# Attention and a routed FFN on one core: rests of the task list after the token choice set to 13 slots and 3 slots

## The chip, the core and the metric

One NeuronCore of a Trainium2 chip runs the whole program in one launch. The metric is the device time of one execution in microseconds (us).

## The reference

Eight batches of 3136 tokens, model width 256. The output of the attention goes through a routed FFN that touches the 128 best tokens of each batch:

```
scores = (z @ z.T) / S                     # z: [8, 3136, 64]
x = u * (max(scores, 0)**2 @ v)            # u, v: [8, 3136, 256]
s = x @ w_gate                             # one score for each token
top = the 128 tokens of a batch with the highest s
h = max(x[top] @ w1, 0)                    # w1: [256, 1024]
x[top] = x[top] + sigmoid(s[top]) * (h @ w2)   # w2: [1024, 256]
```

All products are in float32 accuracy: each operand is split into a high and a low part (names that end in `hi`, `h`, `H` and in `lo`, `l`, `L`), and three products of the parts are summed.

## The kernel before

**Slots.** The work of a batch is cut into 7 chunks of query columns: chunks 0 to 4 have 512 columns, chunk 5 has 256, chunk 6 has 320. Each chunk is worked through in 13 slots, 91 slots for a batch and 728 in all. A slot takes two blocks of 128 keys (the last one of a chunk half a block) and sums their share of the chunk's output on TensorE: the function `mix` issues 12 matmuls (4 in the last slot) at line 521, `acc<-hi,V`, `acc<-lo,V` and `acc<-hi,Vr` by the profile's names. The last slot of a chunk is the one with `Vr`. A slot of 512 columns is long, a slot of chunk 5 is half as long.

**Old and new squares.** The matrix of scores is symmetric. A new pair of key blocks is scored on TensorE (line 415, `sc<-Z,ZH` and `sc<-Z,ZL`), squared on ScalarE and VectorE, and its transposed copy is stored to DRAM (`squares`, `squares_narrow`, `squares_own`). A later chunk fetches that copy instead of computing it (`qk<-squares`, lines 364, 369 and 372), three buffers deep. Chunk 5 and chunk 6 are mostly old squares: they need few scores and many fetches. Scores and squares of a slot are issued three slots ahead of its `mix`.

**Queues.** All plain DMAs of the loop stand in one queue, SyncE's (SP), in program order. SP issues a DMA when what it needs is free or there, and everything behind it waits as well. GpSimd (POOL) issues the two indirect DMAs of the FFN, the gather of the chosen tokens (`xe<-out,ids`) and the scatter of their new values (`out<-y,ids`, line 1158).

**The task list.** Work beside the attention is a list of tasks, `far`. A task has some TensorE operations, which `mix` spreads among the 12 matmuls of a slot, some operations for after that slot, and, as a third member, its rest: the number of slots until the next task of the list may be taken (2 where none is named; 1 in the last batch). At the end of a batch, `route` puts 30 to 40 slots of choosing tokens into the list (counting, then `ahead` at line 795 with `quotas` and `spans`, then `take` at line 836, which needs the spans' result `of` from line 832), and behind that the FFN. So the choice and the FFN of one batch run inside the chunks of the next.

**The FFN.** Its tasks, in order: `number` (the tokens' row numbers; with it SP gets the load of the two halves of w1, 1 MB each, `wh<-w1h_there` and `wl<-w1l_there`, line 185), `gather`, an empty task, `weigh`, the transposition of the tokens (`xeT`, line 1078), six matmuls `h` of 512 columns (line 1104), their transposition `hT` (four matmuls, line 1120), the second six of `h`, then a task that only queues the load of the two halves of w2 into the same two buffers (`wh<-w2h_there`, `wl<-w2l_there`, 1 MB each), the second `hT`, and last 24 matmuls `y` of 256 columns (line 1148) with the scatter. The first four `y` read `wh`, the next four `wl`, and so on.

**Which batches.** The FFNs of batches 0 to 4 run in the next batch in this way. Batches 5 and 6 (`put_off`) only choose, gather and transpose there; their FFNs run at the very end beside that of batch 7, whose routing has rules of its own. So batch 6 runs its seven chunks with no `h`, `hT` and `y` in them.

In batches 1 to 5 the FFN before stands in chunks 3 to 5: `number` at slot 0 of chunk 3, `gather` at slot 3, `weigh` at slot 8, `xeT` at slot 10; the first `h` at slot 0 of chunk 4, `hT` at slot 3, the second `h` at slot 6, the load of w2 behind slot 8, the second `hT` at slot 10; `y` at slot 0 of chunk 5.

Of the kernel before, what the change touches and what calls it, by code (L numbers as in the profile page):

```python
# [85 lines left out]
def attention_then_routed_ffn(ctx: ExitStack, tc: tile.TileContext, zt, ut, v, wg, w1, w2, cst, cst16, keys, outs, at, cap):  # L86
# [260 lines left out]
    def spend(act=0.0, dve=0.0, pool=0.0):  # L347
        busy["act"] += act
        busy["dve"] += dve
        busy["pool"] += pool  # L350
# [187 lines left out]
    def put_off(b):  # L538
        return B - 1 - HELD <= b < B - 1 and merged(B - 1) > 0

    def merged(b):
        return LATE if b == B - 1 and 0 < cap <= P else 0
# [121 lines left out]
    def route(b):  # L664
# [59 lines left out]
        def settle(rd):  # L724
            junk = moe.tile([TP, NS], F32, name="enough", tag="enough")[:R]
            m = moe.tile([TP, 1], F32, name="m", tag="m")[:R]
            nc.vector.tensor_scalar(
                junk, st["ps"][:R, :NS], float(cap), None, op0=ALU.is_ge, op1=ALU.add, accum_out=m
            )
            mi = moe.tile([TP, 1], I32, name="mi", tag="mi")[:R]  # L730
            nc.vector.tensor_copy(mi, m)
            base = moe.tile([TP, 1], I32, name="base", tag="base", bufs=2)[:R]
            if rd == last:
                base = st["ps"][:R, 64:65].bitcast(I32)
            if rd == 0:
                k = moe.tile([TP, 1], I32, name="place", tag="place")[:R]
                nc.vector.tensor_scalar(
                    k, mi, 32 - BITS, INT_MIN, op0=ALU.logical_shift_left, op1=ALU.bitwise_xor
                )
                flip = moe.tile([TP, 1], I32, name="flip", tag="flip")[:R]  # L740
                nc.vector.tensor_scalar(
                    flip, k, 31, 0x7FFFFFFF, op0=ALU.arith_shift_right, op1=ALU.bitwise_and
                )
                nc.vector.tensor_tensor(base, k, flip, op=ALU.bitwise_xor)
            else:
                nc.vector.tensor_scalar(
                    base, mi, 32 - BITS * (rd + 1), st["base"], op0=ALU.logical_shift_left, op1=ALU.bitwise_xor
                )
            st["base"] = base
            spend(dve=0.6)  # L750
# [69 lines left out]
        def spans(r0):  # L820

            rank = consts["rank"][:R, r0 : r0 + P]
            taken, begin, end = st["taken"], st["begin"], st["end"]
            if r0:
                nc.vector.tensor_scalar(taken[:, NT : NT + 1], begin, -float(r0), -2.0 * NT, op0=ALU.add, op1=ALU.max)
                nc.vector.tensor_scalar_min(taken[:, NT : NT + 1], taken[:, NT : NT + 1], 2.0 * P)
            else:
                nc.vector.tensor_scalar_min(taken[:, NT : NT + 1], begin, 2.0 * P)
            upper = moe.tile([TP, P], F32, name="upper", tag="upper")[:R]
            nc.vector.tensor_scalar(upper, rank, end, None, op0=ALU.is_le)  # L830
            of = moe.tile([TP, P], BF16, name="of", tag="big", bufs=2)[:R]
            nc.vector.scalar_tensor_tensor(of, rank, begin, upper, op0=ALU.is_gt, op1=ALU.mult)
            st["of"] = of
            spend(dve=0.6)
# [6 lines left out]
        tasks = [([fold], [start, count], 3)]  # L841
# [4 lines left out]
        if late:  # L846
            tasks.append(([total], [lambda: settle(last), masks]))
            tasks += [([columns], keep_columns), ([places], ranks)]
            tasks += choose(st, 0, cap)
            choice[b] = st  # L850
        else:
            tasks.append(([total], [lambda: settle(last), masks, run_up]))
            tasks.append(([ahead], [quotas, lambda: spans(0)]))
            for r0 in range(0, cap, P):
                n = min(P, cap - r0)
                first, *ffn = expert(b, st, n, r0)
                if put_off(b) and b == B - 2:
                    tasks = [(*t[:2], 2) for t in tasks]
                if r0:
                    tasks.append(([], lambda r0=r0: spans(r0)))  # L860
                tasks.append(([take], None))
                tasks += first
                if put_off(b):
                    held.append(ffn)
                else:
                    tasks += ffn[0] + ffn[1]
# [13 lines left out]
    def choose(st, r0, n):  # L880

        R, NT = st["G"].shape
        QT = Q // 4
        NP = NT // QT

        def pick(q):
            oh = moe.tile([TP, QT, P], BF16, name="oh", tag="big", bufs=2)[:R]
            t = slice(q * QT, (q + 1) * QT)
            nc.vector.tensor_tensor(
                oh,  # L890
                consts["rank"][:R, r0 : r0 + P].rearrange("p (o r) -> p o r", o=1).broadcast_to([R, QT, P]),
                st["rk"][:, t].rearrange("p (t o) -> p t o", o=1).broadcast_to([R, QT, P]),
                op=ALU.is_equal,
            )
            st["oh", q] = oh
            spend(dve=1.1)

        def find(q):
            if q == 0:
                st["ps"] = misc_bank("ids")  # L900
            what = st["what"]
            for i in range(QT):
                t = q * QT + i
                nc.tensor.matmul(
                    st["ps"][:, : what.shape[2]], st["oh", q][:, i, :], what[:, t, :],
                    start=(t == 0), stop=(t == NT - 1),
                )

        def begin():
            tok = consts["tok_half16"][:R].rearrange("p (t w) -> p t w", w=2)  # L910
            what = moe.tile([TP, NT, 5], BF16, name="what", tag="what")[:R]
            nc.vector.tensor_copy(what[:, :, :2], tok)
            cut(st["G"], what[:, :, 2:])
            st["what"] = what
            pick(0)

        tasks = [([], begin), ([], lambda: pick(1))]
        for q in range(NP):
            then = (lambda q=q: pick(q + 2)) if q + 2 < NP else None
            tasks.append(([lambda q=q: find(q)], then))  # L920
        tasks[-1] = (tasks[-1][0], lambda: keep_choice(st))
        return tasks
# [408 lines left out]
    for k, (b, c, js, is_old) in enumerate(slots):  # L1331
# [5 lines left out]
        tasks = []  # L1337
# [58 lines left out]
        if len(js) == 1 and cap > 0:  # L1396
            if c == NCH - 1 - late:
                far.extend([None, *route(b)])
            elif c >= NCH - late:
                last_merge = merge(b, c)  # L1400
                far.extend([None, *last_merge])
                if c == NCH - 1:
                    first, ffn, more = expert(b, choice[b], cap)
# [60 lines left out]
```

## Time and profile before

| | |
|---|---|
| time, median of 3 runs | 2114.52 us (2112.32 to 2115.31) |
| time of the profiled execution | 2112.72 us |
| its span, first to last instruction | 2110.9 us |
| TensorE busy with matmuls | 2081.4 us, 99% of the span |
| VectorE, ScalarE, GpSimd busy | 1559.2, 1263.3, 1313.5 us |
| DMA | 412.01 MB, mean 195 GB/s |
| granted TensorE clock | 1.000 |

A page of the profile names each group of instructions by line, engine, operation and tiles; an arrow `<-` behind a number names what ended a wait. Times in a timeline are us from the start of the span; `x4` behind a row merges four like instructions that follow each other, and the duration is then that of all four. Matmuls overlap each other, so one row's duration is not the distance between two starts.

### The profile page before, as it was taken

How to read it: one execution, taken by the hardware profiler on the slowest of the kernel's cores; microseconds unless marked ns; L12 is line 12 of the kernel's file. 1: busy time of each engine (PE TensorE's matmuls, PEld its weight loads, DVE VectorE, ACT ScalarE, POOL GpSimd, SP SyncE). 2: the span in 40 equal slices, each digit the busy share in tenths (PEclk: the TensorE clock that was granted, in tenths of full speed). 3: DMA queues.
4: the chain of work that ended last, by engine and by line, in shares of the span. 5: the costliest groups of instructions: out<-in, count | busy, mean ns of one | idle time of the engine just before them, and what ended most of it. 6: DMA issues, size and time to landing. Idle time of an engine off the chain costs nothing.

```text
span 2110.9 us, 31339 instructions
## 1 busy us (share of the span) xinstructions
PE 2081.4 (99%) x10359; PEld 1750.4 (83%) x10359; DVE 1559.2 (74%) x2361; ACT 1263.3 (60%) x1570; POOL 1313.5 (62%) x703
## 2 busy tenths in 40 slices
PE   8999999999999999999999999999999999999999
PEld 6788978889888898888888888888888888887788
DVE  8766678775877668776678767787577876788776
ACT  7665576554766457654576546765467654775543
POOL 6676577645766458664587646766467655666643
PEclk9999999999999999999999999999999999999999
DMA  6698766787668766688666876678766776666862
GB/s 189 202 261 222 198 184 173 217 199 213 181 186 218 202 195 190 188 220 220 177 190 187 229 211 173 190 195 217 210 182 185 196 193 171 203 188 162 220 173 96
DMA packets 425730, 412.01 MB, mean 195 GB/s; under 512 B 147616, under 2 KB 338912, under 8 KB 421984
## 3 DMA queue, kind: packets, MB, share of 16 engines
q1 hardware_dynamic: 424512, 407.66, 69.8%
q0 software_dynamic: 768, 2.10, 0.3%
q8 instruction: 81, 1.33, 0.3%
q14 instruction: 81, 0.66, 0.1%
q10 hardware_dynamic: 288, 0.26, 0.0%
HBM read 235.31 MB, written 172.23 MB: 193 GB/s over the span
## 4 chain that ended last, share of the span: by engine, by line
PE 74%; DVE 6%; DMA 6%; ACT 5%; POOL 3%; issue 3%; SPq 2%; POOLq 0%; ACTq 0%; DVEq 0%
PE acc L521 60%; PE sc L415 12%; DVE a L436 2%; POOL lo L485 2%; ACT a L425 2%; ACT hi L426 2%; DMA vst<-in_v 2%; DMA qk<-squares_narrow 1%; DVE aT L454 1%; DMA wl<-w2l_there 1%; DVE lo L485 1%; DMA squares_narrow<-aT 1%; PE h L1104 1%; PE y L1148 1%; SPq L265 0%
## 5 line engine op out<-in xcount | busy, mean ns | idle before, releaser
L521 PE MATMUL acc<-hi,V 128*128 128x512 f32 (+2 forms) x5376 | 1226.0, 366 | 9.0 <-ACT hi L393 4.7
L485 POOL TENSOR_TENSOR lo<-a,hi 128x1024 fp32r<-128x1024 f32 (+2 forms) x327 | 740.8, 2268 | 609.3 <-DVE a L436 438.9
L521 PEld LDWEIGHTS acc<-hi,V 128*128 128x128 f32 x5376 | 930.3, 188 | 175.9 <-DVE ut L566 9.1
L521 PE MATMUL acc<-lo,V 128*128 128x512 f32 (+2 forms) x2688 | 664.2, 364 | 7.2 <-POOL lo L485 3.5
L425 ACT ACTIVATE a<-sc 128x1024 f32<-128x1024 f32 (+4 forms) x408 | 363.2, 890 | 493.2 <-PE sc L415 374.9
L521 PEld LDWEIGHTS acc<-lo,V 128*128 128x128 f32 x2688 | 471.4, 188 | 89.0 <-DVE lo L485 6.4
L436 DVE TENSOR_TENSOR a<-sc,a 128x1024 f32<-128x1024 f32 (+3 forms) x335 | 339.9, 1015 | 258.1 <-ACT hi L426 227.9
L393 ACT CAST hi<-qk 128x1024 fp32r<-128x1024 f32 (+2 forms) x320 | 274.4, 862 | 254.5 <-PE acc L521 204.5
L485 DVE TENSOR_TENSOR lo<-qk,hi 128x1024 fp32r<-128x1024 f32 (+2 forms) x230 | 348.2, 1523 | 84.4 <-ACT hi L393 83.2
L454 DVE STREAM_TRANSPOSE aT<-a 128x512 f32<-128x512 f32 (+1 forms) x520 | 341.0, 691 | 89.5 <-ACT a L431 62.7
L426 ACT ACTIVATE hi<-a 128x1024 fp32r<-128x1024 f32 (+4 forms) x408 | 377.4, 925 | 21.4 <-PE acc L521 5.0
L415 PE MATMUL sc<-Z,ZH 128*128 128x512 f32 (+2 forms) x760 | 280.8, 373 | 3.7 <-DVE a L436 2.1
L415 PE MATMUL sc<-Z,ZL 128*128 128x512 f32 (+2 forms) x760 | 278.2, 370 | 0.7 <-DVE ZL L121 0.7
L485 POOL TENSOR_TENSOR lo<-qk,hi 128x512 fp32r<-128x512 f32 (+2 forms) x90 | 172.9, 1924 | 61.1 <-issue 45.5
L415 PEld LDWEIGHTS sc<-Z,ZH 128*128 128x128 f32 x760 | 142.6, 188 | 35.0 <-DVE a L436 7.7
L415 PEld LDWEIGHTS sc<-Z,ZL 128*128 128x128 f32 x760 | 142.6, 188 | 25.3 <-DVE ZL L121 1.1
L121 POOL TENSOR_TENSOR V<-vst,V 128x512 fp32r<-128x512 f32 x89 | 128.2, 1445 | 28.5 <-ACT V L120 22.4
L587 POOL TENSOR_TENSOR ut<-x,w_run 128x1024 f32<-128x1024 f32 (+2 forms) x52 | 124.3, 2390 | 26.5 <-DVE x L578 25.7
L121 POOL TENSOR_TENSOR ZL<-zst,ZH 128x512 fp32r<-128x512 f32 (+2 forms) x56 | 69.4, 1244 | 17.1 <-ACT ZH L120 17.1
L431 ACT ACTIVATE a<-a 128x1024 f32<-128x1024 f32 x73 | 77.5, 1062 | 2.3
L120 ACT CAST V<-vst 128x512 fp32r<-128x512 f32 x95 | 57.7, 608 | 30.0 <-DMA vst<-in_v 30.0
L566 DVE SCALAR_TENSOR_TENSOR ut<-acc,ut 128x512 f32<-128x512 f32 (+2 forms) x112 | 64.1, 613 | 12.6 <-PE acc L521 12.4
(173 smaller groups left out, 1054.6 us busy)
## 6 DMA issues: line engine op xcount, KB each, us to landing
squares<-aT SPq DMA_DIRECT2D x160, 512.0 KB
qk<-squares SPq DMA_DIRECT2D x320, 256.0 KB
squares_narrow<-aT SPq DMA_DIRECT2D x320, 128.0 KB
qk<-squares_narrow SPq DMA_DIRECT2D x80, 512.0 KB
vst<-in_v SPq DMA_DIRECT2D x190, 128.0 KB
out<-x SPq DMA_DIRECT2D x162, 128.0 KB
ut<-in_ut SPq DMA_DIRECT2D x40, 512.0 KB
squares_own<-aT SPq DMA_DIRECT2D x39, 256.0 KB
```

What stands on the lines that cost most here:

```text
L121: (lo_on or nc.vector.tensor_tensor)(lo, src, hi.bitcast(F32), op=ALU.subtract)
L393: nc.scalar.copy(by(hi), src)
L415: nc.tensor.matmul(ps[:, q], z[:, j * P : (j + 1) * P], mov, start=z is ZH, stop=z is ZL)
L425: nc.scalar.activation(a, ps[:, :n], AF.Relu)
L426: nc.scalar.activation(pieces[0][0](hi), pieces[0][1], AF.Square)
L431: nc.scalar.activation(a, a, AF.Square)
L436: square = lambda: nc.vector.tensor_tensor(a[rows], ps[rows, :n], a[rows], op=ALU.mult)
L454: nc.vector.transpose(to, a[rows, q].rearrange("p (m t a) -> p m t a", t=GT, a=Q))
L485: on.tensor_tensor(view(lo), src, view(hi).bitcast(F32), op=ALU.subtract)
L521: nc.tensor.matmul(ac[h], w, mov, start=first and h not in started, stop=stop)
L566: nc.vector.scalar_tensor_tensor(xT[:, h, :w], acc[b, c][h], SCALE * SCALE, xT[:, h, :w], op0=ALU.mult, op1=ALU.mult)
L587: nc.gpsimd.tensor_tensor(wx, runs, consts["wg_run"].rearrange("p (o r) -> p o r", o=1).broadcast_to([P, NB, RUN]), op=ALU.mult,)
```

## The change

Two rests in the function `route` are set, for all batches but the last. The task `ahead` gets 3 slots of rest in place of 2, and the task `take` gets 13 in place of 2, but stays at 2 where the FFN is put off (batches 5 and 6). For batch 6 the rests of the earlier tasks were set to 2 already, which stays so; its `take`, which runs in the last batch, had the 1 slot of that batch and now has 2.

```
-            tasks.append(([ahead], [quotas, lambda: spans(0)]))
+            tasks.append(([ahead], [quotas, lambda: spans(0)], 3))
...
-                tasks.append(([take], None))
+                tasks.append(([take], None, 2 if put_off(b) else 13))
```

In batches 1 to 5 `take` moves from slot 10 of chunk 2 to slot 11, `number` from slot 0 of chunk 3 to slot 11 of chunk 3, `gather` to slot 0 of chunk 4, `weigh` to slot 6, `xeT` to slot 8, the first `h` to slot 10 of chunk 4; the first `hT` to slot 0 of chunk 5, the second `h` to slot 3, the load of w2 to behind slot 6, the second `hT` to slot 8, and `y` to slot 10 of chunk 5. In batch 6 only `take` moves. The slots of the attention themselves stay as they are.

The end of the FFN on TensorE, before. The rows with 128x512 end chunk 4 (`Vr` is its last slot), those with 128x256 begin chunk 5:

```order
L521 MATMUL acc<-lo,V 128x512 x4
L1120 MATMUL hT<-c_sb,hr 128x128 x4
L521 MATMUL acc<-hi,V 128x512 x8
L521 MATMUL acc<-lo,V 128x512 x4
L521 MATMUL acc<-hi,Vr 128x512 x4
L521 MATMUL acc<-hi,V 128x256 x3
L1148 MATMUL y<-wh,hh 128x256 x2
L521 MATMUL acc<-hi,V 128x256
L1148 MATMUL y<-wh,hh 128x256 x2
L521 MATMUL acc<-lo,V 128x256
L1148 MATMUL y<-wl,hh 128x256 x3
```

The same place of the FFN now, three slots before the end of chunk 5:

```order
L521 MATMUL acc<-lo,V 128x256 x4
L1120 MATMUL hT<-c_sb,hr 128x128 x4
L521 MATMUL acc<-hi,V 128x256 x8
L415 MATMUL sc<-Z,ZH 128x256
L415 MATMUL sc<-Z,ZL 128x256
L521 MATMUL acc<-lo,V 128x256 x4
L521 MATMUL acc<-hi,V 128x256 x3
L1148 MATMUL y<-wh,hh 128x256 x2
L521 MATMUL acc<-hi,V 128x256
L1148 MATMUL y<-wh,hh 128x256 x2
L521 MATMUL acc<-hi,V 128x256
L1148 MATMUL y<-wl,hh 128x256 x3
```

The matmuls `y` moved from the first slot of chunk 5 to its eleventh, and all slots between the load of w2 and `y` are now slots of 256 columns.

On SP, the queue of plain DMAs, before, from the end of chunk 4 on. `squares_narrow_4` are stores of chunk 4, `qk<-squares_narrow_2`, `_3` and `_4` fetches for chunk 5, `out<-x` the output of chunk 4, `Z<-ZH` and `Z<-ZL` the columns of chunk 6, the later `qk` rows fetches for chunk 6, `ut` the input u for chunk 5:

```order
L468 DMA squares_narrow_4_111<-aT 32x4x256 x4
L185 DMA wh<-w2h_there 128x2048
L185 DMA wl<-w2l_there 128x2048
L468 DMA squares_narrow_4_111<-aT 32x4x128 x2
L369 DMA qk<-squares_narrow_2_107 128x2x512
L369 DMA qk<-squares_narrow_3_109 128x2x512
L223 DMA zst<-in_zt 64x512 x2
L369 DMA qk<-squares_narrow_4_111 128x2x512
L585 DMA out<-x 32x16x64 x4
```

The same queue now, from that `out<-x` on:

```order
L585 DMA out<-x 32x16x64 x4
L265 DMA Z<-ZH 64x4x32 x2
L267 DMA Z<-ZH 64x64
L265 DMA Z<-ZL 64x4x32 x2
L267 DMA Z<-ZL 64x64
L369 DMA qk<-squares_narrow_0_103 128x2x512
L372 DMA qk<-squares_narrow_0_103 128x256
L185 DMA wh<-w2h_there 128x2048
L185 DMA wl<-w2l_there 128x2048
L556 DMA ut<-in_ut 128x2x256
L369 DMA qk<-squares_narrow_1_105 128x2x512
L372 DMA qk<-squares_narrow_1_105 128x256
```

The load of w2 moved back past the fetches and stores of chunk 5 and past the first fetch for chunk 6; before, the `ut` row followed that fetch directly.

The load of w1 on the same queue, as a difference, in chunk 3 and at the start of chunk 4:

```order
-L185 DMA wh<-w1h_there 128x2048
-L185 DMA wl<-w1l_there 128x2048
 L364 DMA qk<-squares_2_106 32x4x512 x4
 L460 DMA squares_3_108<-aT 512x1x256
@@ -172,4 +170,6 @@
 L468 DMA squares_narrow_3_109<-aT 32x4x128 x2
 L364 DMA qk<-squares_2_106 32x4x512 x4
+L185 DMA wh<-w1h_there 128x2048
+L185 DMA wl<-w1l_there 128x2048
 L475 DMA squares_own_4_121<-aT 128x512
 L383 DMA vst<-squares_own_4_121 32x4x128 x4
```

It moved from before the third fetch of chunk 3 to before the store and the fetch back of `squares_own` of chunk 4.

## The prediction

> **What bounds the kernel now.** I read the page first, then TensorE's waits, then a table of stretches, then the timeline around the FFN. The page:
>
> ```profile
> span 2110.9 us, 31339 instructions
> PE 2081.4 (99%) x10359; PEld 1750.4 (83%) x10359; DVE 1559.2 (74%) x2361; ACT 1263.3 (60%) x1570; POOL 1313.5 (62%) x703
> PEclk9999999999999999999999999999999999999999
> ```
>
> TensorE is the bound in every stage, at the full clock, so the change can win only what TensorE waits for today and lose only by new waits. The waits (total us, times, longest), TensorE's and those of engines that feed it:
>
> ```profile
> PE acc L521 <- POOL lo L485: 3.5, 3, 2.4
> PE y L1148 <- DMA wl<-w2l_there: 1.6, 3, 0.8
> PEld L838 <- DVE of L832: 3.6, 6, 0.6
> PE taken L838 <- DVE of L832: 1.1, 6, 0.2
> ACT hi L393 <- DMA qk<-squares_narrow: 28.5, 12, 3.8
> POOL out L1158 <- DVE y L1154: 31.5, 8, 7.2
> ```
>
> Two of them belong to tasks that move: `take` waits for the spans six times, `y` waits for w2 three times. Now the stretches in which the FFN stands. The first six rows run from the first matmul of chunk 4 to the end of chunk 6, for batches 1 to 6; the last two are chunk 4 alone, of batch 1 and of batch 6. The first number behind the window is its length.
>
> ```profile
> 440.33:532.34 92.01, 90.00 (x536) 80.42 (x535) 58.37 (x65) 46.43 (x67) 46.12 (x27) 1.00 0.69 189
> 701.01:791.60 90.59, 89.73 (x535) 80.46 (x534) 58.72 (x65) 46.39 (x67) 45.52 (x27) 1.00 0.68 194
> 960.28:1052.36 92.08, 89.47 (x535) 80.43 (x534) 59.53 (x65) 46.50 (x67) 45.33 (x27) 1.00 0.67 191
> 1220.98:1312.54 91.56, 89.53 (x535) 80.46 (x534) 59.37 (x65) 46.50 (x67) 45.33 (x27) 1.00 0.66 188
> 1481.18:1573.36 92.18, 89.40 (x536) 80.47 (x535) 59.07 (x65) 46.60 (x67) 46.56 (x27) 1.00 0.70 193
> 1742.24:1824.72 82.48, 82.28 (x494) 74.58 (x493) 53.53 (x63) 44.62 (x64) 46.56 (x26) 1.00 0.66 181
> ...
> 440.33:480.51 40.18, 40.18 (x183) 33.11 (x182) 26.28 (x28) 18.54 (x23) 17.71 (x9) 1.00 0.74 201
> 1742.20:1779.30 37.10, 36.98 (x166) 30.23 (x164) 24.36 (x27) 16.55 (x20) 18.97 (x9) 1.00 0.66 175
> ```
>
> Batch 6 has no `h`, `hT` and `y` in these chunks and is the yardstick. Both `h` and both `hT` cost chunk 4 40.18 - 37.10 = 3.1 us. The 24 `y` start 0.12 us apart (the rows of batch 3 below), 2.9 us. So three chunks with an FFN would take 82.5 + 3.1 + 2.9 = 88.5 us if they waited no more than batch 6 does. They take 91.7 on average: 3.2 us a batch are waits, a little of it at `y`, the rest in chunk 6, whose fetches come late (the 28.5 us of casts that wait for `qk<-squares_narrow`). These 3.2 us, five times, are all that a better place of the FFN could win here.
>
> **The load of w2, the part that decides.** Before, it is queued behind slot 8 of chunk 4 and has long slots in front of `y`; now the slots between are short ones. First where it lands today, in batches 1, 5 and 3:
>
> ```profile
> 473.72 0.39 SPq L185 DMA_DIRECT2D wh<-w2h_there  x1
> 497.97 0.52 SPq L369 DMA_DIRECT2D qk<-squares_narrow  x1
> ...
> 482.19 0.62 PE L1148 MATMUL y<-wl,hh 128*128 128x256 f32 x3 [0.45 <-DMA wl<-w2l_there]
> ...
> 502.37 1.36 ACT L393 CAST hi<-qk 128x640 fp32r<-128x640 f32 x2 [2.14 <-DMA qk<-squares_narrow]
> ...
> 1514.68 0.40 SPq L185 DMA_DIRECT2D wh<-w2h_there  x1
> ...
> 1523.50 0.62 PE L1148 MATMUL y<-wl,hh 128*128 128x256 f32 x3 [0.78 <-DMA wl<-w2l_there]
> ...
> 993.79 0.39 SPq L185 DMA_DIRECT2D wh<-w2h_there  x1
> ...
> 1001.74 0.62 PE L1148 MATMUL y<-wl,hh 128*128 128x256 f32 x3
> 1002.20 0.28 PE L521 MATMUL acc<-lo,V 128*128 128x256 f32 x1
> 1002.32 0.28 PE L1148 MATMUL y<-wl,hh 128*128 128x256 f32 x1
> 1002.44 0.28 PE L1148 MATMUL y<-wh,hh 128*128 128x256 f32 x1
> ```
>
> From the issue of `wh` to the moment at which `wl` is there it takes 482.19 - 473.72 = 8.5 us in batch 1 and 8.8 in batch 5; in batch 3 nothing waits 7.95 us after it, so it landed before that. Now when it will be issued, and when `y` will be reached, counted from the first matmul of chunk 5. Batch 6 is again the pattern, because nothing of an FFN delays its chunk 5:
>
> ```profile
> 1779.30 0.64 PE L521 MATMUL acc<-hi,V 128*128 128x256 f32 x4
> ...
> 1794.89 1.12 PE L521 MATMUL acc<-hi,V 128*128 128x256 f32 x8
> ...
> 1791.87 0.52 SPq L369 DMA_DIRECT2D qk<-squares_narrow  x1
> ...
> 1793.00 0.38 SPq L556 DMA_DIRECT2D ut<-in_ut  x1
> ...
> 453.50 0.60 PE L1120 MATMUL hT<-c_sb,hr 128*128 128x128 f32 x4
> 453.86 1.39 PE L521 MATMUL acc<-hi,V 128*128 128x512 f32 x5
> ```
>
> - *When TensorE reaches the first `wl`.* Slot 10 begins at 1794.89 - 1779.30 = 15.6. In front of it now stand two `hT` of 453.86 - 453.50 = 0.36 each and one set of `h`, (3.1 - 0.7) / 2 = 1.2: together 1.9, so 17.5. Five matmuls of the slot and four `y` on `wh` come first, 9 x 0.12 = 1.1: `wl` is needed at 18.6.
> - *When w2 is issued.* It now stands directly before `ut`, which SP issues at 1793.00 - 1779.30 = 13.7 in batch 6. SP's rows in front of it follow TensorE's first slots through the output of chunk 4 and a fetch, so some of the added 1.9 delays them: between 13.7 and 15.6. I take 14.3, since of the added work only the first `hT` (0.36) lies in front of the slots that these rows follow.
> - *When it lands.* 8.5 us later as in batch 1, and later by what is queued directly in front: the first fetch for chunk 6, 0.6 MB, whose reader in batch 1 waited until 502.37, 4.4 us after the issue at 497.97. I add 0.8 (an estimate; 0 to 2 are possible): 9.3, and `wl` is there at 23.6.
>
> The Trainium skill ("DMA: Bandwidth & Descriptors", section "Queues, rings and completion order") says that an engine consumes its descriptors in ring order, so w2 starts only behind that fetch. The cast's late release at 502.37 agrees; no view shows single descriptors. Without that rule the 0.8 falls away, and `wl` is there at 22.8.
>
> So TensorE stands still for 23.6 - 18.6 = 5.0 us in each of five batches, in two parts: about half until `wh` is there, then, four `y` later, until `wl` is. Bounds: 13.7 + 7.95 - 18.6 = 3.1 and 15.6 + 8.8 + 2 - 18.6 = 7.8. The short waits at `y` of today are part of the 3.2 us.
>
> **What that stall gives back.** While TensorE stands, the fetches for chunk 6 go on. The first is queued ahead of w2 and no longer late. The others stand behind 2 MB more, some 7 us; but TensorE gets to chunk 6 later as well, counted from their issue: by the 2.9 of `y`, which now lie behind that issue and not ahead of it, and by the stall of 5.0. That is 7.9 against 7, so chunk 6 should wait no more than in batch 6, and the 3.2 us go. Three chunks then take 88.5 + 5.0 = 93.5 in place of 91.7: +1.8 us, five times, +9 us.
>
> **The other parts.** *`ahead` with 3 slots*: `take` gets a long slot more, and its wait for `of` ends. It is between 1.1 (PE) and 3.6 us (PEld) by the rows above; I take -2.0. *`number`, `gather`, `weigh`, `xeT`, first `h`*: the same instructions with the same distances, hidden beside TensorE as before; 0. *The load of w1* moves to chunk 4, ahead of the store of `squares_own` and its fetch back:
>
> ```profile
> 443.13 0.34 SPq L475 DMA_DIRECT2D squares_own<-aT  x1
> ...
> 447.01 1.73 SPq L383 DMA_DIRECT2D vst<-squares_own  x4
> ...
> 457.68 0.61 ACT L428 CAST hi<-vst 128x512 fp32r<-128x512 f32 x1
> ```
>
> SP waits 447.01 - 443.13 = 3.9 us for the store to land; behind 2 MB of w1 it could be up to 8.5 us later. The cast that needs the fetch comes 8.9 us after 448.74, its end of issue, so the load hides, barely; the stores and fetches queued behind it have slots in hand. Without this cover it is up to 1 us a batch; I take 0 and chunk 3 gains nothing. *The scatter* moves with `y`: GpSimd and VectorE stand behind it until `y` is done (31.5 us in all for the eight, longest 7.2), now longer, and the first low parts of chunk 6 stand behind it on VectorE; two slots lie between, which covers them. 0 to 0.5 us a batch, taken at 0. *Batch 6's choice in the last batch* moves by one slot; 0, at most a few tenths either way.
>
> **Sum.** +9 - 2 = +7 on the profiled execution's 2112.7: 2119.7. The median of the runs shown lies 1.8 above that execution, so 2121.5; I predict 2121. A measurement of this kernel can tell about 0.2%, 4.2 us, from no change.
>
> **Rivals.**
>
> - *The load lands early (faster).* The stall replaces 3.2 us of waits; with w2 at 14.0 and landing after 7.0 us it ends at 21.0, a stall of 2.4. Then 88.5 + 2.4 is 0.8 below today, -4 - 2 = -6: 2108 beside the median. It decides from `wl` at 21.3 on downwards. For it: batch 3 shows only that 7.95 us is enough. Against it: batches 1 and 5 with 8.5 and 8.8, and the fetch in front. Chance 0.14. The Trainium skill's fit for one transfer ("DMA: Bandwidth & Descriptors", section on the anatomy of one DMA), 2 us and the bytes at 436 GB/s, would give 6.8 us for the 2.1 MB; it is for GpSimd's path, and batches 1 and 5 disagree.
> - *It balances (within 0.2%).* A stall of 3 to 4 us, near the lower bound, cancels against the 3.2 and the 2 of `take`: about 2114. Chance 0.26.
> - *Nothing is given back (much slower).* If the late transfers of chunk 6 keep their 3.2 us because 2 MB more stand in front of them, a batch loses 5.0: +25 - 2, 2137. Chance 0.10. The waits of batch 6, with the same fetches, speak against it.
> - *The clock falls.* Two waits of 2 to 3 us close together could let the granted clock drop; if the rest of slot 10, 3.4 us of work, then takes twice as long, that is +3.4 a batch on top, 17 in all, 2138. Against it: a wait of 2.4 us stands among TensorE's today (the first row of the waits) and PEclk shows 9 throughout. Chance 0.08. This is the rule of the Trainium skill ("TensorE: Matmul & The Clock Gate", Part 1): half rate after an idle window of about 3.4 us; no run here shows such a window inside the kernel.
>
> **Numbers.** The forecast, a stall of 4 to 6.5 us against 3.2 us given back, has 0.42 and a range of its own from 2116 to 2129. Slower: 0.42 + 0.10 + 0.08 = 0.60; within 0.2%: 0.26; faster: 0.14. The range goes from 2109, just above the early landing, to 2136, the upper bound of the stall (4.6 x 5 - 1).
>
> **What would show it.** Right: `y` waits for `wh` and `wl` about 5 us in each of five batches, at slot 10 of chunk 5; w2 is issued 14 to 15 us after the chunk's first matmul; the casts' wait for `qk<-squares_narrow` falls well below 28.5 us; `taken` waits no more; chunks 4 to 6 take 93 to 94 us. Wrong: `y` waits under 3 us, or chunk 6 of those batches still waits for its fetches, or the clock shows digits below 9.

## The result, and the profile after

The changed kernel takes 2136.18 us (median of 5 runs, 2135.44 to 2139.04), the kernel before 2114.74 us beside it (5 runs, 2112.32 to 2118.62). The ratio is 1.0109, with a 95% interval from 1.0097 to 1.0122: 21 us slower, where 7 had been forecast. The profiled execution took 2135.44 us; its span is 22.7 us longer than that of before. All lines here are of it unless another kernel is named. First the page:

```profile
span 2133.6 us, 31351 instructions
PE 2088.7 (98%) x10359; PEld 1760.5 (83%) x10359; DVE 1537.0 (72%) x2356; ACT 1265.1 (59%) x1570; POOL 1324.5 (62%) x708
PEclk9999999999999999999999999999999999999999
```

TensorE has the same 10359 matmuls and is busy 7.3 us longer with them (2081.4 before). That is the first sign that some of them ran slower, although every digit of the clock is a 9: a slice of this page is 53 us long, and 7 us at half clock take less than a tenth from it. The waits that answer to those shown of before:

```profile
PE y L1148 <- DMA wh<-w2h_there: 15.2, 5, 4.1
PE y L1148 <- DMA wl<-w2l_there: 5.8, 5, 1.5
ACT hi L393 <- DMA qk<-squares_narrow: 19.7, 3, 9.1
```

`y` now waits for both halves of w2 in all five batches, 21.0 us in sum where it was 1.6. The wait of `taken` for the spans is gone, and the casts wait 19.7 us for their fetches where they waited 28.5. Of these, 9.1 and 8.5 us fall into slot 10 of chunk 5 of batches 2 and 4, while TensorE itself stands there, and 2.1 into batch 6, which has no FFN; in chunk 6 of batches 1 to 5 no cast waits for such a fetch any more. Now the stretch from the first matmul of chunk 4 to the end of chunk 6, batches 1 to 5; the number behind POOL's busy time and count is the granted clock:

```profile
439.50:535.80 96.30, 91.86 (x537) 83.04 (x536) 59.63 (x71) 48.42 (x70) 48.51 (x29) 0.96 0.70 205
703.93:801.64 97.71, 91.88 (x537) 83.02 (x536) 57.24 (x71) 47.25 (x69) 48.87 (x29) 0.97 0.69 200
969.71:1065.56 95.85, 90.93 (x537) 82.06 (x536) 57.01 (x71) 47.16 (x69) 49.41 (x29) 0.98 0.70 204
1233.66:1330.78 97.12, 91.81 (x538) 82.97 (x536) 58.03 (x71) 47.04 (x69) 49.42 (x29) 0.96 0.68 203
1498.82:1595.39 96.57, 91.00 (x537) 81.98 (x536) 58.32 (x71) 47.05 (x69) 48.82 (x29) 0.98 0.70 203
```

The mean is 96.7 us, against 91.7 before and 93.5 forecast, and the clock column reads 0.96 to 0.98 where before it read 1.00. Slot 10 of chunk 5, the slot with `y`, in batch 2, first SP's issues and then TensorE:

```profile
757.08 0.38 SPq L185 DMA_DIRECT2D wh<-w2h_there  x1
757.50 0.43 SPq L185 DMA_DIRECT2D wl<-w2l_there  x1
```

```profile
760.23 0.52 PE L521 MATMUL acc<-hi,V 128*128 128x256 f32 x3
764.84 0.58 PE L1148 MATMUL y<-wh,hh 128*128 128x256 f32 x2 [4.10 <-DMA wh<-w2h_there]
...
767.23 1.01 PE L1148 MATMUL y<-wl,hh 128*128 128x256 f32 x3 [0.95 <-DMA wl<-w2l_there]
768.04 0.41 PE L521 MATMUL acc<-hi,V 128*128 128x256 f32 x1
768.25 0.41 PE L1148 MATMUL y<-wl,hh 128*128 128x256 f32 x1
```

Two waits, as forecast, and behind them matmuls of the same shape that last 0.41 us and start 0.21 us apart, where in the batch shown of before they lasted 0.28 and started 0.12 apart. The slot, which takes 4.27 us where nothing in it waits (the early load of w2 below), takes 12.37 here. In the five batches it takes 10.81, 12.37, 10.17, 11.74 and 10.21, mean 11.06.

The clock itself is seen only in stretches as short as its own steps. Its records say 0.5 once in each of the five batches, for 3.41 or 6.83 us, and these spells begin a whole number of 3.413 us apart (498.82 and 765.06: 78 steps). So the table below is cut on that grid; the columns are length, busy time of PE, PEld, DVE, ACT and POOL, the granted clock, the DMA share and GB/s:

```profile
495.41:498.82 3.41, 0.90 (x8) 0.69 (x6) 1.06 (x3) 0.80 (x2) 1.50 (x2) 1.00 1.04 426
498.82:502.24 3.42, 2.43 (x10) 2.17 (x10) 0.00 (x0) 0.00 (x0) 0.00 (x0) 0.50 1.01 396
502.24:505.65 3.41, 3.41 (x17) 3.41 (x17) 0.00 (x0) 0.73 (x1) 0.00 (x0) 0.50 0.77 275
...
761.65:765.06 3.41, 0.22 (x2) 0.25 (x3) 0.18 (x1) 0.00 (x0) 0.00 (x0) 1.00 0.95 378
765.06:768.47 3.41, 2.46 (x12) 2.16 (x12) 0.00 (x0) 0.00 (x0) 0.00 (x0) 0.50 1.04 392
768.47:771.89 3.42, 3.42 (x18) 3.42 (x18) 0.00 (x0) 0.73 (x1) 0.00 (x0) 0.50 0.31 112
...
1024.47:1027.89 3.42, 2.04 (x18) 1.83 (x16) 1.81 (x4) 1.39 (x3) 2.66 (x2) 1.00 1.05 425
1027.89:1031.30 3.41, 0.95 (x6) 0.77 (x6) 0.00 (x0) 0.00 (x0) 0.00 (x0) 1.00 1.00 402
1031.30:1034.71 3.41, 3.34 (x15) 3.34 (x16) 0.00 (x0) 0.59 (x1) 0.00 (x0) 0.50 0.98 352
1034.71:1038.13 3.42, 3.42 (x31) 3.42 (x30) 1.22 (x2) 0.87 (x2) 1.01 (x1) 1.00 0.01 3
```

A step at full clock in which TensorE is busy 0.2 to 0.95 us is followed by one at 0.50; if that one holds the second wait (busy 2.43 and 2.46), the next is at 0.50 too; a step busy for 2.04 us is followed by the full clock. The Trainium skill ("TensorE: Matmul & The Clock Gate", Part 1) says that the clock is halved after an idle window of about 3.4 us and that these windows run free of the program. The grid agrees. A window need not be wholly idle here: 0.95 us of work in it did not keep the clock.

### The profile page after: what moved, and what is told of

Read it like the earlier page. It is cut to its first block, busy times and chain, and to the rows that moved or that the text cites. A ratio compares the mean times of both kernels' runs of the same rounds, so it can differ in the third digit from the quotient of the medians.

```text
span 2133.6 us, 31351 instructions
## 1 busy us (share of the span) xinstructions
PE 2088.7 (98%) x10359; PEld 1760.5 (83%) x10359; DVE 1537.0 (72%) x2356; ACT 1265.1 (59%) x1570; POOL 1324.5 (62%) x708
## 4 chain that ended last, share of the span: by engine, by line
PE 77%; DMA 8%; DVE 5%; ACT 4%; issue 2%; SPq 2%; POOL 2%; POOLq 0%; DVEq 0%; ACTq 0%
PE acc L521 63%; PE sc L415 12%; DMA wl<-w2l_there 2%; DMA vst<-in_v 2%; ACT a L425 2%; DVE a L436 2%; POOL lo L485 1%; ACT hi L426 1%; DMA squares_narrow<-aT 1%; DMA ut<-in_ut 1%; PE y L1148 1%; DVE lo L485 1%; PE h L1104 1%; DVE aT L454 1%; DMA qk<-squares 1%
## 5 line engine op out<-in xcount | busy, mean ns | idle before, releaser
L426 ACT ACTIVATE hi<-a 128x1024 fp32r<-128x1024 f32 (+4 forms) x408 | 377.7, 926 | 17.8 <-PE acc L521 1.2
L485 DVE TENSOR_TENSOR lo<-qk,hi 128x1024 fp32r<-128x1024 f32 (+2 forms) x225 | 328.9, 1470 | 78.4 <-ACT hi L393 68.9
L485 POOL TENSOR_TENSOR lo<-qk,hi 128x1024 fp32r<-128x1024 f32 (+2 forms) x95 | 182.7, 1926 | 46.4 <-ACT hi L393 28.2
```

The costliest lines, as they stand in the source:

```text
L426: nc.scalar.activation(pieces[0][0](hi), pieces[0][1], AF.Square)
L485: on.tensor_tensor(view(lo), src, view(hi).bitcast(F32), op=ALU.subtract)
```

## The experiments

The theory after the first result: w2 is queued too near to `y`; the stall itself came as forecast, and what is lost beyond it is TensorE at half clock behind it. Rivals: another part of the change loses (the rests, w1, the new place), or the half clock is only a mark in the records.

The table holds all kernels; the first runs of the two that were run twice stand in the text. "Slot with y" is the mean length of that slot in batches 1 to 5, from the first matmul of the slot to that of the next. The runs came in three groups, each with the kernel before run beside it (2115.19, 2114.04 and 2114.27 us); the ratio is to those. A spare pair is one spare matmul of the kernel, which the profile shows as two.

| kernel | FFN | w2 queued behind | slot with y, us | time, us | ratio, 95% interval |
|---|---|---|---|---|---|
| before | old place | chunk 4, slot 8 | 5.29 | 2114.7 | |
| changed | new place | chunk 5, slot 6 | 11.06 | 2136.2 | 1.0097 to 1.0122 |
| rest of `ahead` alone | old | chunk 4, slot 8 | 5.43 | 2112.8 | 0.9979 to 0.9999 |
| w2 late alone | old | chunk 4, slot 10 | 9.82 | 2134.5 | 1.0072 to 1.0105 |
| w2 early (second run) | new | chunk 5, slot 3 | 4.69 | 2104.2 | 0.9933 to 0.9964 |
| old place, w2 early (second run) | old | chunk 4, slot 6 | 4.73 | 2111.2 | 0.9971 to 0.9991 |
| 13 spare pairs | new | chunk 5, slot 6 | 10.59 | 2134.2 | 1.0073 to 1.0114 |
| 22 spare pairs | new | chunk 5, slot 6 | 9.88 | 2130.8 | 1.0067 to 1.0098 |
| `wl` last | new | chunk 5, slot 6 | 9.12 | 2123.1 | 1.0025 to 1.0054 |
| rest 8 | between | chunk 5, slot 0 | 5.52 | 2119.7 | 1.0016 to 1.0035 |
| w2 early, `wl` last | new | chunk 5, slot 3 | 4.27 | 2105.5 | 0.9941 to 0.9970 |

**Half of the change: `ahead` alone.** Of the change only this line is made:

```
-            tasks.append(([ahead], [quotas, lambda: spans(0)]))
+            tasks.append(([ahead], [quotas, lambda: spans(0)], 3))
```

> The first half of the change alone: ahead with 3 slots of rest, take with its 2 as before. Theory (the loss is the load of w2 that comes too late in front of y, and TensorE's clock that falls in that wait; the longer rest of ahead is a small gain): 2 us below the kernel before, 2112 to 2113, no wait of taken for of, clock 1.000. Rival (the longer rest itself disturbs something): at or above the kernel before.

2112.79 us (10 runs, 2108.52 to 2116.24), 2.4 less than before beside it. Chunk 2, where `take` stands, lasts 40.85 us in place of 41.18, six times: 2.0 us. The first line of the change gains what was forecast, though the interval reaches from nearly nothing to twice that; the loss belongs to the second.

**Only the lateness of w2, in the kernel before.** The FFN stays where it stood; the load is queued two slots later:

```
+        late_ops, late_post = tur[1]
-        return first, [], [hid[0], tur[0], hid[1], ([], lambda: bring_weight(2)), tur[1], (to_y, scatter)]
+        return first, [], [hid[0], tur[0], hid[1], ([], None), (late_ops, [late_post, lambda: bring_weight(2)]), (to_y, scatter)]
```

> The kernel before, with the load of w2 queued two slots later, behind the second hT, and nothing else moved: the FFN stays in its old place. Theory (load of w2): w2 is issued about 3.8 us later than in the kernel before, y waits 4 us in each of five batches, +18 to 20 us, and if the clock falls there too 5 to 12 more: 2143, from 2130 to 2150. Rival (the FFN's new place is the cost, not the load): 2115.

2134.47 us (4 runs, 2131.55 to 2143.23; the profiled execution is the longest of them), below the 2143 expected but within its range: nearly the whole loss without any of the change. TensorE's waits, and steps of the clock's grid in batches 1 and 2:

```profile
PE y L1148 <- DMA wl<-w2l_there: 7.4, 5, 1.6
PE y L1148 <- DMA wh<-w2h_there: 6.9, 5, 1.6
```

```profile
485.05:488.46 3.41, 1.45 (x10) 1.28 (x11) 0.00 (x0) 0.00 (x0) 0.90 (x1) 1.00 0.98 399
488.46:491.87 3.41, 3.41 (x18) 3.41 (x18) 0.00 (x0) 0.60 (x1) 0.00 (x0) 0.50 0.70 240
747.88:751.29 3.41, 1.59 (x11) 1.17 (x9) 1.16 (x2) 0.62 (x1) 1.79 (x2) 1.00 0.99 417
751.29:754.70 3.41, 2.44 (x11) 2.44 (x12) 0.00 (x0) 0.00 (x0) 0.00 (x0) 0.50 1.03 365
```

No single wait is longer than 1.6 us, and yet the clock is halved in every batch: the two waits leave 0.94 to 1.59 us of work in a step. Only the load moved here, so its distance to `y` is what costs.

**Only the lateness of w2 taken back, in the changed kernel.** The load goes behind the second `h`, an empty task takes its old place:

```
-        return first, [], [hid[0], tur[0], hid[1], ([], lambda: bring_weight(2)), tur[1], (to_y, scatter)]
+        return first, [], [hid[0], tur[0], (hid[1][0], [hid[1][1], lambda: bring_weight(2)]), ([], None), tur[1], (to_y, scatter)]
```

> The changed kernel, with the load of w2 queued directly behind the second h (slot 3 of chunk 5) and not three slots later; all other tasks keep their slots. Theory (load of w2): w2 is issued about 8.5 us after the first matmul of chunk 5 and there at 17.5 to 18.5, y waits less than 1 us, the clock stays at 1.000, slot 10 falls from 11 us to about 4.5: 5 x 6.6 = 33 us less, 2103, or up to 2110 if chunk 6 gets its waits back. Rival (the new place of the FFN among the short slots of chunk 5 costs by itself, on the engines that feed TensorE): stays above 2125.

2105.65 us (4 runs, 2102.14 to 2106.30): the loss is gone and 9 us are won. So the rests, w1 and the new place together lose nothing that shows. SP issues w2 8.3 to 8.7 us after the first matmul of chunk 5 in place of 14.4 to 15.1. In batches 1 and 5 the first `y` with `wl` still waits 0.7 us.

**The half clock, with 13 spare matmuls.** In the changed kernel, ahead of the first `y`, whose result overwrites theirs:

```
+                for _ in range(0 if roomy else 13):
+                    nc.tensor.matmul(st["ps"][:, :P], consts["ident"], consts["ones"], start=True, stop=True)
```

> The changed kernel, with 13 spare matmuls of 128 columns (constants, about 0.21 us each, 2.8 us in all) between the third matmul of slot 10 and the first y in each of the five batches, whose result y overwrites. They keep TensorE busy in the time in which it waits for wh. Theory with the clock as a cost of its own: the clock stays at 1.000, the waits for w2 fall to 1 to 2.5 us, and the 2.4 us a batch that the half clock cost go: 2124, from 2120 to 2128. Rival (the half clock costs nothing, since the time is set by the landing of w2 alone): 2136 as before or above.

2134.18 us (4 runs, 2131.70 to 2139.17): outside the range expected, and inconclusive as a time. In batches 1, 2 and 5 the clock stayed full, in batches 3 and 4 it fell. With 3.1 us of spare work both waits remain in batches 2, 3 and 4 (1.1 to 1.4 us and 1.5 to 2.1 us), and batch 2 kept its clock all the same. Two steps of this run, each with the one behind it, show how little decides:

```profile
763.26:766.67 3.41, 1.70 (x14) 1.70 (x15) 0.00 (x0) 0.10 (x1) 0.00 (x0) 1.00 0.89 331
766.67:770.08 3.41, 3.41 (x31) 3.41 (x31) 1.22 (x2) 1.24 (x2) 0.84 (x1) 1.00 0.12 43
1026.09:1029.50 3.41, 1.33 (x9) 1.14 (x10) 0.00 (x0) 0.00 (x0) 0.00 (x0) 1.00 1.04 379
1029.50:1032.91 3.41, 3.41 (x19) 3.41 (x18) 0.00 (x0) 0.73 (x1) 0.00 (x0) 0.50 0.29 105
```

**The half clock, with enough spare work.** The same with 22 in place of 13:

> The changed kernel with 22 spare pairs of matmuls of 128 columns (about 5.2 us, result overwritten) ahead of the first y of batches 0 to 4, so that TensorE works through the wait for wh and nearly all of that for wl. Theory (after the wait TensorE runs at half clock, and that costs about 2.4 us a batch): the granted clock stays at 1.0 in batches 1 to 5, slot 10 of chunk 5 lasts 9.5 to 10.2 us in place of 11.1, and the time is about 2130 us. Rival (the half clock is a mark in the records and costs nothing): slot 10 lasts 11 us or more, 2136 us or above.

2130.84 us (4 runs, 2129.09 to 2131.72), 5.3 less than the changed kernel, and no step at 0.50 in the whole run. Slot 10 lasts 9.16, 10.88, 9.81, 10.28 and 9.28 us. Batch 2 again, whose clock is 1.00 now; the first number of the first row is the start of slot 10, the window ends with the slot:

```profile
757.64:768.52 10.88, 9.42 (x82) 9.22 (x81) 0.85 (x2) 1.25 (x3) 1.16 (x1) 1.00 0.81 308
```

```profile
758.00 5.07 PE L1146 MATMUL y<-c_sb 128*128 128x128 f32 x44
762.83 0.48 PE L1150 MATMUL y<-wh,hh 128*128 128x256 f32 x2
...
765.24 0.62 PE L1150 MATMUL y<-wl,hh 128*128 128x256 f32 x3 [1.46 <-DMA wl<-w2l_there]
```

From the first `wl` to the end of the slot it takes 768.52 - 765.24 = 3.28 us. In the changed kernel's batch 2 it took 772.60 - 767.23 = 5.37 for the same matmuls, 5.08 on the mean of the five. So the half clock is time, not only a mark: 1.8 us a batch. The rival is out. That the whole time falls by 5.3 us and not by 9 fits with a cost of the spare work itself: the first `y` with `wl` starts 6.61 us behind the start of the slot on the mean, where it starts 5.98 behind it without.

**One wait in place of two.** In the changed kernel the eight `y` that read `wl` are put behind all the others but one:

```
+        to_y = [*to_y[:4], *to_y[8:12], *to_y[16:23], *to_y[4:8], *to_y[12:16], to_y[23]]
```

> The changed kernel with the matmuls y in another order: all but one of the sixteen products with wh first, then the eight with wl, then the last one with wh. The first wait, for wh, stays; the second, for wl (1.5 us or less), is covered by some 2.6 us of work at full clock. Theory A (the two waits together let the clock fall): the clock stays at 1.0, slot 10 lasts 7.3 to 8.3 us in place of 11.1, 2118 to 2122 us. Theory B (the first wait alone lets it fall): the clock is at 0.5 for 3.4 us behind the wait in each batch, slot 10 lasts about 9 to 9.7 us, 2125 to 2129 us.

2123.10 us (5 runs, 2119.64 to 2125.82), between the two ranges expected. The wait for `wh` is as before, that for `wl` is gone, and the clock is at 0.50 for one step in every batch. Batch 2, the step with the wait and the one behind it, and the line of the waits:

```profile
760.13:763.54 3.41, 0.04 (x1) 0.07 (x1) 0.42 (x2) 0.00 (x0) 0.08 (x1) 1.00 0.99 399
763.54:766.95 3.41, 3.41 (x16) 3.41 (x17) 0.00 (x0) 0.00 (x0) 0.00 (x0) 0.50 1.03 386
```

```profile
PE y L1148 <- DMA wh<-w2h_there: 15.7, 5, 4.3
```

By the clock and by the slot's 9.12 us theory B had it: the first wait alone lets the clock fall. The second wait, with the second step at half clock in the batches that had one, cost 13 us of the changed kernel's 21 by the medians (10 us by the two profiled executions), for which an order of matmuls was enough.

**Another distance.** In the changed kernel `take` rests 8 slots:

```
-                tasks.append(([take], None, 2 if put_off(b) else 13))
+                tasks.append(([take], None, 2 if put_off(b) else 8))
```

> The changed kernel with 8 slots of rest behind take in place of 13: w2 is queued behind slot 0 of chunk 5 and y stands in slot 6, with five short slots between in place of three. Theory (the load of w2 is too near to y): w2 is issued about 4 us after the first matmul of chunk 5, wl is there about 9 us later, at 13; TensorE would need it at 10.4, so a stall of 2 to 3 us in place of 4.4, in the short waits mostly too short for the clock to fall: 2112 to 2120 us. Rival (short slots of chunk 5 are a bad place for y whatever the distance): 2130 us or more.

2119.72 us (9 runs, 2117.05 to 2121.92): the time was as expected, but by luck, as the way was not. SP issues w2 0.9 us after the first matmul of chunk 5 and not 4, and the slot with `y` takes 5.52 us on the mean, a stall of some 1.2 and not 2 to 3. What costs here is chunk 4, which lasts 41.0 to 44.9 us (40.3 before, with the same two `h` in it). TensorE's waits, then SP's issues and VectorE in batch 3, say why:

```profile
PE acc L521 <- DVE ut L566: 6.7, 6, 2.9
```

```profile
948.61 0.38 SPq L185 DMA_DIRECT2D wh<-w1h_there  x1
949.03 0.43 SPq L185 DMA_DIRECT2D wl<-w1l_there  x1
949.56 0.69 SPq L556 DMA_DIRECT2D ut<-in_ut  x1
```

```profile
967.14 1.29 DVE L566 SCALAR_TENSOR_TENSOR ut<-acc,ut 128x512 f32<-128x512 f32 x2 [2.67 <-DMA ut<-in_ut]
```

With this rest the 2 MB of w1 stand directly ahead of `ut`, the input that chunk 3's output is multiplied with; in batch 3 it is there only 17.6 us after its issue, and chunk 4 waits for that; in that batch the step with this wait, 0.84 us of work, is followed by one at half clock too. The change itself puts w1 elsewhere and pays nothing for it. This cause is read from the trace; it was not tried by itself, and in the other batches, where chunk 4 is 0.7 to 1.5 us longer, it is only the likeliest.

**What the new place is worth.** The old place with `ahead` at 3 and the same early load:

> The FFN stands where it stood before, ahead has 3 slots of rest, and the load of w2 is queued behind slot 6 of chunk 4 in place of slot 8; nothing else differs. Theory (w2's lead before y is all that the place of the FFN is worth): the short waits at y go (1.6 us in the kernel before), and the time comes down to that of the kernel with the early load in the new place, about 2106 us. Rival (the new place itself relieves chunk 6, whose fetches then do not compete with w2): chunk 6 keeps its 27.5 to 29 us and chunks 4 to 6 stay at 91 us or more; only the wait of take is won, 2111 to 2113 us.

2108.77 us (11 runs, 2106.50 to 2113.38), between the two theories. Its profiled execution was the fastest but one of its runs and made the old place look as good as the new one. So both were run on one chip:

> The changed kernel with the load of w2 queued behind the second h, once more, now on one chip with the same early load in the old place, to tell what the place of the FFN is worth with w2 out of the way. In the profiles chunks 4 to 6 took 90.5 us here and 90.4 us there. Theory (the place is worth nothing by itself): both come out within 2 us of each other. Rival (the new place is worth some 3 us, as the medians of two calls had it, 2105.7 against 2108.8): this one is faster by 3 us.

> The FFN in its old place, ahead with 3 slots of rest, w2 queued behind slot 6 of chunk 4; the other half of that comparison. Theory: within 2 us of the new place. Rival: slower than it by 3 us.

2104.17 us (5 runs, 2101.64 to 2106.55) in the new place, 2111.15 (11 runs, 2107.14 to 2113.54) in the old. The rival holds: the new place is faster, by 7 us side by side and by 3 between the medians of the earlier runs, which were not on one chip. The 7 are more than the place explains: of the 8.0 us between the two profiled executions 4.8 lie in batches 1 to 5 and 3.7 in batches 0 and 6, which run no FFN (the tail takes 0.6 back). In the old place the last slot of chunk 5 lasts 0.50 to 2.47 us where it is 0.48 in the new one, since casts for chunk 6 come late; in the old place's batch 4:

```profile
1281.20 1.35 ACT L393 CAST hi<-qk 128x640 fp32r<-128x640 f32 x2 [3.95 <-DMA qk<-squares_narrow]
```

TensorE stands behind this cast, and the next step runs at half clock. With `y` late in chunk 5 its 2.9 us seem to give these fetches time; that is read from the traces and was not tried by itself. This relief is smaller than what the late load takes.

**Both cures together**, the early load and `wl` last:

> The new place with the early load and with the y that read wl put last (all but one of the products with wh first). With the early load alone, the first y of wl still waited 0.7 us in two of five batches. Theory: that wait goes too, slot 10 lasts 4.3 us in every batch, 1 to 2 us are won, about 2104 us. Rival (the order of y costs something of its own, for instance by waiting for the low parts of h): slot 10 is longer than 4.3 us and nothing is won.

2105.45 us (5 runs, 2103.71 to 2107.07). The slot lasts 4.27 us in all five batches, as expected, but the 1 to 2 us do not show in the time; the interval overlaps that of the early load alone. The best version stays the change with the early load: 2104.2 us, 0.5% below before and 1.5% below the change.

## Why the prediction was wrong

Right in sign, wrong in size: 2121 was forecast and 2136.2 measured, a hair above the range's upper end of 2136. The step that failed is the clock behind the stall, which the sum put at nothing and which cost 1.8 us a batch; beside it the yardstick, batch 6, was 1.4 us too low.

- *When w2 is issued, and when TensorE needs it.* 14.3 and 17.5 us after the first matmul of chunk 5 were forecast; w2 came 14.4 to 15.1 after it and slot 10 began 17.8 after it (760.23 - 742.47 in batch 2). Right.
- *When it lands.* 9.3 us after its issue were forecast; `y` with `wl` starts 8.28, 10.15, 8.70, 9.56 and 8.56 us after it, mean 9.05. Right; the spread of 2 us was named as the unknown.
- *The stall.* `wl` was forecast 6.1 us behind the start of slot 10 in place of 1.1, a stall of 5.0. It was there 5.64, 7.00, 5.38, 6.37 and 5.49 us behind it, mean 5.98: a stall of 4.9. Right. (The view of waits shows 4.2, as it counts only the time after a matmul's modelled end.)
- *The clock: this step failed.* The sum put it at nothing. The rival stood at 0.08, with the argument that "a wait of 2.4 us stands among TensorE's today" and the clock shows 9 throughout. It happened in each of the five batches and cost 1.8 us a batch, shown with 22 spare pairs; 3.4 a batch had been given for the whole rest of the slot. The argument failed because what counts is the work left in one step of 3.41 us, and the two waits of this stall leave 0.2 to 0.95. The wait of 2.4 us, in chunk 0 of batch 0, was a lucky one: it stands in all 13 kernels, 2.3 to 2.8 us long and always near 63.5 us, and the clock is halved behind it in nine of them. Where the grid lay in the trace of before, the step kept 2.08 us of work; in the kernel with `ahead` alone it kept 0.81:

```profile
61.99:65.40 3.41, 2.08 (x8) 1.42 (x9) 3.38 (x5) 1.06 (x2) 3.41 (x2) 1.00 0.59 187
65.40:68.81 3.41, 3.41 (x17) 2.78 (x16) 1.46 (x3) 1.70 (x2) 2.52 (x2) 1.00 0.61 181
```

```profile
60.41:63.82 3.41, 0.81 (x4) 0.39 (x3) 2.97 (x5) 2.54 (x3) 2.65 (x2) 1.00 0.36 114
63.82:67.24 3.42, 3.42 (x9) 2.63 (x9) 2.07 (x4) 0.83 (x1) 3.42 (x2) 0.50 0.51 148
```

  And the page's digits could not have shown such spells at all.
- *What the stall gives back: the term was mis-sized.* "Chunk 6 should wait no more than in batch 6", whose 26.5 us came from one batch of one trace. Chunk 6 takes 27.3, 27.1, 27.5, 27.2 and 28.2, mean 27.45: better than the 28.1 before, but 1.0 above that yardstick. The yardstick itself was low: batch 6 of the changed kernel, with no FFN, takes 27.3 there, and in the 13 traces its chunk 6 takes 26.3 to 28.5. Against its own trace the argument held. Nor did the 3.2 us stand where the prediction had them, all but a little in chunk 6: before, 0.6 a batch stood at `y` (5.29 against 4.73 without a wait), 1.0 in the last slot of chunk 5 (1.48 against 0.48) and 1.6 in chunk 6. The first two went, and 0.6 of the third. With w2 early chunk 6 takes the same 27.5, so the late w2 is not what it waits for. In batch 2 it loses its time at slot 9, where a low part is late:

```profile
793.74 0.85 PE L521 MATMUL acc<-lo,V 128*128 128x320 f32 x4 [0.62 <-DVE lo L485]
```

```profile
787.83 0.62 ACT L120 CAST V<-vst 128x512 fp32r<-128x512 f32 x1 [1.85 <-DMA vst<-in_v]
```

  ScalarE stands there at the casts of v for the next batch, whose loads come late, and its later casts with it. That is only read from the trace; what sets chunk 6 stays open.
- *The floor.* 88.5 us was 0.4 too low: chunks 4 and 5 take 62.45 without waits (the early load), 62.0 were in the sum.
- *`ahead`, w1, the scatter.* -2 was forecast for `ahead`, measured so by itself. w1 and the scatter cost nothing that shows: with the early load both stand as in the change and it is faster than before.

Together, per batch: 93.5 + 1.8 (clock) + 1.0 (chunk 6) + 0.4 (floor) = 96.7, as measured. Over five batches the misses are 16 us, and +7 becomes +23; the spans differ by 22.7.

The rival that nothing is given back named the right time, 2137, for a wrong reason: chunk 6 did get shorter. The rival of the clock, 2138, named it too, partly by luck: its mechanism was right, but its price was nearly double, and the short yardstick made up the difference.

## What to carry to other kernels

When a stage is moved, its loads move with it: count the time, not the slots, between where a load is queued and where it is needed, and queue it as soon as its buffer is free. A stall of TensorE can cost more than its length, as here the clock was halved behind it, so look at the clock in stretches of a few us, since the page averages it away; two stalls close together can be made one by putting last what arrives last. A yardstick from one batch of one trace has a spread of its own: look at it in more than one before a sum rests on it. A good place with a late load can look like a bad place: undo the load alone before the place is judged.

## What the runs showed of the hardware

- In the 13 profiles the granted clock changes only on a grid of 3.413 us. Cut on this grid, they hold 29 steps at full clock that half clock follows. Every step with up to 1.6 us of TensorE work by the profile was one of them, and none with 1.94 or more. Between lies no sharp bound: steps with 1.70, 1.74, 1.75, 1.80, 1.84 and 1.91 kept the clock, and in the old place with w2 early (its first run) one with 1.93 did not:

```profile
1277.99:1281.40 3.41, 1.93 (x13) 1.47 (x12) 1.29 (x2) 1.35 (x2) 0.00 (x0) 1.00 0.99 316
1281.40:1284.81 3.41, 3.41 (x15) 3.41 (x14) 1.99 (x5) 2.06 (x3) 0.00 (x0) 0.50 0.93 336
```

- A step at half clock was followed by another one where it held up to 2.78 us of work (six times), and by the full clock from 2.96 on (29 times).
- While w2 is on its way the DMA engines are full: in the changed kernel's steps above the DMA share is 0.95 to 1.05 at 378 to 426 GB/s until it has landed. In the kernel before it is 0.99 at 347 GB/s between issue and landing in batch 1. So the 8 to 10 us from issue to landing there are more likely a matter of the bytes in the queue at that time than a fixed delay; that is read from the share, not tried.
